# Attention, mixer and MLP on one core: where the output projection is staged, and how many attention outputs are buffered

## The chip, the cores and the metric

One core of a Trainium2 chip runs the whole program in one launch. The metric is the device time of an execution in microseconds (us); the kernel before has a median of 846.66 us over six runs (845.64 to 852.13).

## What is computed

The input x has 2048 rows of 576 numbers. After a layer norm, two branches are computed, and the output is x plus their product:

```python
xn = _layernorm(x, axis=-1)
s = _A_ref(xn, A_k_cache, A_v_cache, A_wq, A_wo)                # attention
g = _silu(_B_ref(xn, B_w1, B_w2, B_w3, B_w4))                   # mixer and MLP
return x + s * g
```

Branch A: queries `xn @ wq` for 32 heads of width 128; two query heads share one of 16 K and V heads; only the last 512 cached positions are used; softmax; the heads' outputs, side by side, times `wo` (4096 x 576). Branch B: a second layer norm, `gelu(... @ w1)`, four column groups of it shifted by 1 or 2 rows up or down, `@ w2`, plus its input (this is x1); then layer norm, `gelu(... @ w3)` to 4608 columns, `@ w4`, plus x1.

## The kernel before, in words

The rows are worked on in NB = 4 blocks of QB = 512 (TB = 4 tiles of 128 rows). Stage A (lines 216 to 697) does attention, the output projection and the mixer for all blocks; stage B (lines 700 to 991) does the MLP and the final product, with s, g and x1 passed through DRAM.

**The head loop.** Stage A is one loop over u = 0 ... 127 (line 679), u = 32 * block + head; "head u" below is a turn of it. The order on SP, POOL and TensorE is the order of the program (`manual_schedule`, line 662); VectorE and ScalarE are ordered by the framework's priorities, where `high_priority` (lines 391, 423, 501 and others) lets work in front. One turn runs:

- `stage_s(u, 0..3)` (line 398): four score products `sc` and on ScalarE four exponentials into `pT`;
- `stage_q(u + 1)` (line 382): the next head's query, five products `psq`, and its copy to qT, by VectorE in block 0 and by ScalarE in the others;
- `stage_v(u - 1)` (line 410), in two halves: 16 products `po` of 129 columns (the last is the row sum) into one of two PSUM buffers; VectorE takes the reciprocal (L424) and writes the scaled result into `o` (L425), a tile of `o_pool`, which has 4 buffers;
- `stage_t(u - 1)` (line 430): a DMA transpose on SP's queue, `oT<-o` (L433). `oT_pool` has 36 tiles. When it has landed, the `o` buffer is free.

**Filler.** Two tables put other work in: `fill` (`at`, `later`) for what is not TensorE's and `pe_fill` (`pe`) for TensorE's, which is cut into thirds behind the turn's later score products. Lines 615 to 659 are a timetable by head:

- the output projection of block b - 1 (`wo_atoms`, line 438), five groups at heads base + 1 to base + 5 of block b: four of 32 products `pswo`, each followed by a ScalarE copy (L454), and one of 128 narrow products `pswr` for the last 64 columns (copy L461), then the store of the tile `s_out` to s_dram (L462), on SP's queue, for the last block on ScalarE's. It reads the 32 oT of its block;
- the mixer's layer norm at base + 7 (`ln2_steps`), its transposes `xnnT<-xnn_b` (`tr2`, L357) on SP's queue at base + 10 to 13, its first product `b1` (`ph`, L492) from base + 15 or 17 on, which needs all four;
- `b2_shift` and `b2` (L543), which write x1 into a tile of `x1_pool` (2 buffers) that is stored to x1_dram (L570);
- the next block's x loads, layer norm (`ln1_steps`) and transposes `xT_b<-xn_b` (`tr1`, L357). For block 1 the layer norm starts at head 20 and the transposes stand at heads 23 to 26;
- loads on POOL's queue, some gated (`late`, line 303) by a small POOL copy that waits for a given head's first exponential: `load_wo(i)` for head 4 + 3i, and `load_wq`, `load_v`, `load_k`, which wait for their buffer.

`x1_pool` is used in turn for four K loads (`load_k`, block 0), for x1 of each block (line 535), and for x1 read back (`load_x1`). `hb_pool` (2 buffers) holds the mixer's gelu output `hb` of each block. `so_pool` has one buffer, for `s_out`.

Of the kernel before, what the change touches and what calls it, by code (L numbers as in the profile page):

```python
# [8 lines left out]
P = 128  # L9
# [3 lines left out]
BF16 = mybir.dt.bfloat16  # L13
# [18 lines left out]
def kernel(  # L32
# [18 lines left out]
    _, S, D = A_x.shape  # L51
# [10 lines left out]
    QB = 512  # L62
    NB = S // QB
    TB = QB // P
# [11 lines left out]
    PAD = 2  # L76
# [19 lines left out]
    def rows(ap, t0, n):  # L96
        return ap[t0 * P:(t0 + n) * P, :].rearrange("(tt p) d -> p tt d", p=P)
# [98 lines left out]
    x1_pool = ctx.enter_context(tc.tile_pool(name="x1_pool", bufs=2))  # L196
# [19 lines left out]
    with ExitStack() as actx:  # L216
        def pool(name, bufs, space=None):
            kw = {} if space is None else {"space": space}
            return actx.enter_context(tc.tile_pool(name=name, bufs=bufs, **kw))
# [14 lines left out]
        xraw = pool("xraw", 4)  # L234
        qT_pool = pool("qT_pool", 3)
        pT_pool = pool("pT_pool", 10)
        o_pool = pool("o_pool", 4)
        hb_pool = pool("hb_pool", 2)
        hs_pool = pool("hs_pool", 1)
        g1_pool = pool("g1_pool", 1)  # L240
        so_pool = pool("so_pool", 1)
        oT_pool = pool("oT_pool", 36)
        wo_sb = pool("a_wo", 1).tile([P, Hq, D], BF16, name="wo_sb")

# [8 lines left out]
        def load_x(b, eng):  # L253
            x_t[b] = []
            for tt in range(TB):
                xt = xraw.tile([P, D], BF16, name="xt")
                t = b * TB + tt
                eng.dma_start(out=xt[:], in_=x2[t * P:(t + 1) * P, :])
                x_t[b].append(xt)
# [43 lines left out]
        def late(ap, fn):  # L303
            g = nc.gpsimd.tensor_copy(out=gate[:, :], in_=ap)
            with tc.issue_after(g.ins):
                fn()
# [49 lines left out]
        def transpose_tile(dstT, src, tt):  # L356
            nc.sync.dma_start(out=dstT[:, :, tt * P:(tt + 1) * P], in_=src[:, tt, :], transpose=True)  # L357
# [14 lines left out]
        def tr1(b, tt):  # L372
            transpose_tile(xT_b[b % 2], xn_t[b], tt)
# [62 lines left out]
        so_t = {}  # L436

        def wo_atoms(qb):
            psp, tag = (ps_pq, "pq") if qb == NB - 1 else (ps_wo, "wo")
            groups = []  # L440
            st = {}

            def mm(ps, h, tt, lo, hi):
                nc.tensor.matmul(ps, lhsT=oT_t[qb * Hq + h][:, tt, :], rhs=wo_sb[:, h, lo:hi], start=(h == 0),  # L444
                                 stop=(h == Hq - 1))

            def main(tt, h):
                if tt == 0 and h == 0:
                    so_t[qb] = so_pool.tile([P, TB, D], BF16, name="s_out")
                if h == 0:  # L450
                    st["ps"] = psp.tile([P, M0], FP32, name="pswo", tag=tag)
                mm(st["ps"][:, :], h, tt, 0, M0)
                if h == Hq - 1:
                    nc.scalar.activation(out=so_t[qb][:, tt, 0:M0], in_=st["ps"][:, :], func=ACT.Copy, scale=0.5)  # L454

            def rem(tt, h):
                if tt == 0 and h == 0:
                    st["pr"] = psp.tile([P, TB, R0], FP32, name="pswr", tag=tag)
                mm(st["pr"][:, tt, :], h, tt, M0, D)
                if tt == TB - 1 and h == Hq - 1:  # L460
                    nc.scalar.activation(out=so_t[qb][:, :, M0:D], in_=st["pr"][:, :, :], func=ACT.Copy, scale=0.5)  # L461
                    (nc.scalar if qb == NB - 1 else nc.sync).dma_start(out=rows(s_dram, qb * TB, TB),  # L462
                                                                       in_=so_t.pop(qb)[:])

            for tt in range(TB):
                groups.append([lambda tt=tt, h=h: main(tt, h) for h in range(Hq)])
            groups.append([lambda tt=tt, h=h: rem(tt, h) for tt in range(TB) for h in range(Hq)])
            return groups

# [3 lines left out]
        def ln2_steps(b):  # L473
            return layernorm_steps(small, [xnn_b[:, tt, 0:D] for tt in range(TB)],
                                   [xn_t[b][:, tt, 0:D] for tt in range(TB)])

        def tr2(b, tt):
            transpose_tile(xnnT, xnn_b, tt)

        def b1(b, c):  # L480
            st = {}

            def mm(kc):
                if kc == 0:
                    if c == 0:
                        hb_t[b] = hb_pool.tile([P, 5, QB + 2 * PAD], BF16, name="hb")
                        if b == 0:
                            nc.vector.memset(hb_t[b][:, :, 0:PAD], 0.0)
                        if b == NB - 1:
                            nc.vector.memset(hb_t[b][:, :, PAD + QB:], 0.0)  # L490
                    st["ph"] = ps_pq.tile([P, QB], FP32, name="ph", tag="pq")
                nc.tensor.matmul(st["ph"][:, :], rhs=xnnT[:, kc, :],  # L492
                                 lhsT=w1r_sb[:, kc, :] if c == 4 else w1_sb[:, kc, c * c4:c * c4 + P],
                                 start=(kc == 0), stop=(kc == NDC - 1))
                if kc == NDC - 1:
                    gelu1(b, c, st["ph"])

            return [lambda kc=kc: mm(kc) for kc in range(NDC)]
# [25 lines left out]
        def b2_shift(b):  # L524
            with tc.high_priority(offset=HP):
                b2_shift_(b)
# [18 lines left out]
        def b2(b, tt):  # L545
            st = {}

            def mm(c):
                if c == 0:
                    st["ps"] = ps_wo.tile([P, M0], FP32, name="psx1", tag="wo")  # L550
                b2_mm(st["ps"][:, :], b, tt, c, 0, M0)
                if c == 4:
                    with tc.high_priority(offset=HP):
                        nc.vector.tensor_tensor(out=x1o_t[b][:, tt, 0:M0], in0=st["ps"][:, :],
                                                in1=xn_t[b][:, tt, 0:M0], op=ALU.add)

            return [lambda c=c: mm(c) for c in range(5)]
# [38 lines left out]
        def at(u, fn):  # L596
            fill.setdefault(u, []).append(fn)

        def pe(u, atoms):
            pe_fill.setdefault(u, []).extend(atoms)  # L600
# [5 lines left out]
        def later(u, make, per):  # L606
            cell = []
            for i in range(2 * TB + 1):
                def step(i=i):
                    if not cell:  # L610
                        cell.append(make())
                    cell[0][i]()
                at(u + i // per, step)

        for b in range(NB):
            base = b * Hq
            if b > 0:
                for i, group in enumerate(wo_atoms(b - 1)):
                    pe(base + 1 + i, group)
            later(base + 7, lambda b=b: ln2_steps(b), 3)  # L620
            for tt in range(TB):
                at(base + 10 + tt, lambda b=b, tt=tt: tr2(b, tt))
            for c in range(5):
                pe(base + (15 if 0 < b < NB - 1 else 17) + c, b1(b, c))
            for bb in ([b - 1] if b > 0 else []) + ([b] if b == NB - 1 else []):
                o2 = base + (28 if bb == b else 23 if b == NB - 1 else 21)
                at(o2 - 1, lambda bb=bb: b2_shift(bb))
                for tt in range(TB):
                    pe(o2 + tt, b2(bb, tt))
                pe(o2 + 3, b2_rem(bb))  # L630
            if b + 1 < NB:
                at(base + (8 if b == 0 else 4), lambda b=b: late(pT_t[b * Hq + (8 if b == 0 else 4)][0][0:1, 0:1],
                                                                 lambda: load_x(b + 1, nc.gpsimd)))
                u1 = base + (24 if b else 20)
                later(u1, lambda b=b: ln1_steps(b + 1), 3)
                for tt in range(TB):
                    at(u1 + (3 + tt // 2 if b else 3 + tt), lambda b=b, tt=tt: tr1(b + 1, tt))
        for i, group in enumerate(wo_atoms(NB - 1)):
            pe(U + 1 + i, group)
        at(2, lambda: late(pT_t[2][0][0:1, 0:1], load_w1))  # L640
# [59 lines left out]
    with ExitStack() as bctx:  # L700
# [181 lines left out]
        with tc.manual_schedule(engines={PE, DVE, ACTE}):  # L882
# [7 lines left out]
            for d in range(0, ND, 2):  # L890
                b = d // NP
# [4 lines left out]
                if end:  # L896
                    assert not work
                    bs = bs_pool.tile([P, TB, D], FP32, name="bs")
                    x1 = x1_t[b]
# [48 lines left out]
            b = NB - 1  # L948
# [34 lines left out]
            tt = TB - 1  # L983
# [11 lines left out]
    with tc.If(flag > 0):  # L995
        with ExitStack() as gctx:
# [19 lines left out]
            with tc.For_i(0, NT, 1) as t:  # L1016
# [10 lines left out]
                for h in range(Hq):  # L1027
                    g = h // REP
                    if h % REP == 0:
                        k_nat = work.tile([P, KCH, Dh], BF16, name="r_k")  # L1030
                        nc.sync.dma_start(out=k_nat[:],
                                          in_=A_k_cache[0, g, K0:, :].rearrange("(kc p) d -> p kc d", p=P))
                        v_g = work.tile([P, KCH, Dh], BF16, name="r_v")
                        nc.sync.dma_start(out=v_g[:],
                                          in_=A_v_cache[0, g, K0:, :].rearrange("(kc p) d -> p kc d", p=P))
# [16 lines left out]
                    p = work.tile([P, W], BF16, name="r_p")  # L1052
# [63 lines left out]
```

## Time and profile before

| what | us |
|---|---|
| median of the six runs | 846.66 |
| the six runs | 845.66, 845.64, 847.04, 850.60, 852.13, 846.27 |
| the profiled execution | 858.82 |
| its span, first to last instruction | 857.0 |
| TensorE busy in it | 829.6 |
| ScalarE, VectorE, POOL busy | 461.0, 426.1, 76.7 |

The profiled execution is longer than all six runs shown; times below that come from it are its own. Its mean granted TensorE clock is 0.992.

How such a page is read: a group's line gives source line, engine, operation, output<-input by the program's names, shapes and count, then busy time and mean ns of one, then the idle time of the engine just before these instructions and what ended most of it. "SPq" is a DMA issue on SyncE's queue. A line of waits gives who waited for whom, then total us, times and the longest. A line of the timeline gives the start, the length, the engine and the operation, merged where equal ones follow each other; in brackets stands the idle time before it and what ended it. "DMA to landing" is the time from a transfer's issue to its arrival.

In the stretch of stage A over blocks 1 to 3 (180 to 566 us) TensorE's waits for other engines and DMAs add up to 1 us, and in stage B, from 566 us to the last products, to 0.2 us. Of the transposes `oT<-o` the median lands 3.0 us after its issue, the longest 17.4; of `xnnT<-xnn_b` 5.4 and 19.6.

### The profile page before, as it was taken

The page shows a single profiled execution, that of the slowest core. Times are in us where ns is not written, and L with a number is a line of the kernel's source. Part 1 is how long each engine was busy: PE and PEld are TensorE (multiplying, and loading weights), DVE is VectorE, ACT ScalarE, POOL GpSimd, SP SyncE. Part 2 cuts the span into 40 slices and gives each one's busy share as a digit, 9 for nine tenths or more (in the row PEclk, how much of TensorE's full clock was granted, in tenths as well). Part 3 has the DMA queues.
Part 4 walks back from the last instruction along what each step waited for, and adds up shares of the span by engine and source line. Part 5 has one row for each costly group of instructions (what it writes and reads, how often), then busy time and mean ns, then how long its engine had stood idle before and what let it go on. Part 6 is the DMA issues. An engine that isn't in the chain of part 4 may idle for free.

```text
span 857.0 us, 19361 instructions
## 1 busy us (share of the span) xinstructions
PE 829.6 (97%) x7896; PEld 487.1 (57%) x7980; DVE 426.1 (50%) x1351; ACT 461.0 (54%) x825; POOL 76.7 (9%) x134
## 2 busy tenths in 40 slices
PE   8978989999999999999999999999999999999996
PEld 6645655566565566565466556455555555555554
DVE  5755961156772145873126686025236636655333
ACT  5754774378885368877359876023333424334610
POOL 3431210310101101010001000000000000000000
PEclk9998999999999999999999999999999999999999
DMA  7997582245355137245128424995001321230101
GB/s 179 220 191 128 148 160 58 71 102 116 93 112 92 47 87 130 66 121 96 41 60 138 99 66 98 255 329 144 2 2 43 53 77 43 39 92 15 44 15 45
DMA packets 139983, 83.94 MB, mean 98 GB/s; under 512 B 106944, under 2 KB 133248, under 8 KB 139888
## 3 DMA queue, kind: packets, MB, share of 16 engines
q1 hardware_dynamic: 130048, 53.01, 30.8%
q0 software_dynamic: 8448, 28.15, 12.3%
q10 hardware_dynamic: 1392, 1.48, 0.5%
q8 instruction: 64, 1.05, 0.5%
q14 instruction: 31, 0.25, 0.1%
HBM read 49.17 MB, written 9.44 MB: 68 GB/s over the span
## 4 chain that ended last, share of the span: by engine, by line


## 5 line engine op out<-in xcount | busy, mean ns | idle before, releaser
L405 ACT ACTIVATE pT<-sc 128x512 bf16<-128x512 f32 x512 | 290.4, 596 | 115.6 <-PE sc L403 100.3
L403 PE MATMUL sc<-qT,kT 128*128 128x512 bf16 x493 | 176.3, 381 | 1.3 <-DVE qT L393 0.6
L420 PEld LDWEIGHTS <-pT 128*128 128x128 bf16 x2048 | 140.8, 98 | 62.7 <-DVE o L425 12.4
L420 PE MATMUL po<-v_sb,pT 128*128 128x129 bf16 x2048 | 163.2, 222 | 12.4 <-DVE o L425 10.9
L388 PE MATMUL psq<-xT_b,wq_b 128*128 128x512 bf16 x603 | 152.0, 379 | 2.8 <-DMA xT_b<-xn_b 0.7
L424 DVE RECIPROCAL ri_b<-po 128x2 f32<-128x2 f32 x256 | 42.9, 168 | 190.4 <-PE po L420 186.5
L769 PE MATMUL ph<-xT_b,w_s 64*128 64x512 bf16 x976 | 127.1, 376 | 0.0
L806 PE MATMUL pm<-w_s,h 64*128 64x512 bf16 x864 | 122.3, 377 | 0.0
L425 DVE TENSOR_TENSOR o<-po,ri_b 128x256 bf16<-128x256 f32 x256 | 107.7, 421 | 24.1 <-DMA oT<-o 17.7
L444 PE MATMUL pswo<-wo_sb,oT 128*128 128x512 bf16 x497 | 114.2, 379 | 0.8
L787 ACT ACTIVATE h<-ph 128x512 bf16<-128x512 f32 x67 | 39.4, 597 | 130.5 <-PE ph L769 130.5
L388 PEld LDWEIGHTS <-wq_b 128*128 128x128 bf16 x640 | 62.5, 98 | 75.3 <-issue 3.5
L806 PEld LDWEIGHTS <-h 64*128 64x128 bf16 x1728 | 70.8, 94 | 55.6 <-issue 0.4
L444 PEld LDWEIGHTS <-oT 128*128 128x128 bf16 x1024 | 64.9, 98 | 55.2
L806 PE MATMUL pr<-w_s,h 64*128 64x64 bf16 x864 | 90.2, 189 | 0.2 <-ACT h L787 0.2
L769 PEld LDWEIGHTS <-w_s 64*128 64x128 bf16 x1152 | 57.2, 94 | 48.2 <-issue 0.2
L395 ACT ACTIVATE qT<-psq 128x512 bf16<-128x512 f32 x96 | 57.4, 598 | 28.4 <-PE psq L388 27.0
L785 DVE COPY hx<-ph 128x512 f32<-128x512 f32 x55 | 38.0, 691 | 69.3 <-PE ph L769 69.3
L403 PEld LDWEIGHTS <-kT 128*128 128x128 bf16 x512 | 47.7, 98 | 28.4 <-DVE qT L393 1.2
L265 POOL DMA_DIRECT2D wq_b<-in_A_wq_dram x30 | 23.4, 778 | 315.4 <-PE psq L388 296.1
L787 ACT ACTIVATE h<-hx 128x512 bf16<-128x512 f32 x55 | 34.6, 630 | 7.9 <-DVE hx L785 6.0
L759 DVE TENSOR_SCALAR fence<-ph,ph 1x1 f32<-1x1 f32 x61 | 12.8, 209 | 51.2 <-PE ph L769 50.6
(122 smaller groups left out, 643.0 us busy)
## 6 DMA issues: line engine op xcount, KB each, us to landing
wq_b<-in_A_wq_dram POOLq DMA_DIRECT2D x30, 512.0 KB, 5.4
w_s<-in_B_w_dram SPq DMA_DIRECT2D x9, 576.0 KB, 6.9
wo_sb<-in_A_wo_dram POOLq DMA_DIRECT2D x8, 576.0 KB, 5.2
w_s<-in_B_w_dram SPq DMA_DIRECT2D x9, 512.0 KB, 7.8
x_dram<-x SPq DMA_DIRECT2D x4, 576.0 KB, 3.5
x<-x_dram SPq DMA_DIRECT2D x4, 576.0 KB, 5.3
s_b<-s_dram SPq DMA_DIRECT2D x4, 576.0 KB, 5.3
x_b<-in_A_x_dram SPq DMA_DIRECT2D x4, 576.0 KB, 5.6
```

The costliest lines, as they stand in the source:

```text
L388: nc.tensor.matmul(psq[:, :], lhsT=w[:, kc, hh * Dh:(hh + 1) * Dh], rhs=xT_b[qb % 2][:, kc, :], start=(kc == 0), stop=(kc == NDC - 1))
L395: nc.scalar.activation(out=qT[:, :], in_=psq[:, :], func=ACT.Copy)
L403: nc.tensor.matmul(sc[:, :], lhsT=kT[:, g, kc * P:(kc + 1) * P], rhs=qT_t[u][:, :], start=True, stop=True)
L405: nc.scalar.activation(out=pT[:, :], in_=sc[:, :], func=ACT.Exp, scale=SCALE)
L420: nc.tensor.matmul(po[:, j, :], lhsT=pTs[kc][:, tt * P:(tt + 1) * P], rhs=v_sb[:, g, kc, 0:Dh + 1], start=(kc == 0), stop=(kc == KCH - 1))
L424: nc.vector.reciprocal(out=ri, in_=po[:, :, Dh])
L425: nc.vector.tensor_tensor(out=o[:, t0:t0 + 2, :], in0=po[:, :, 0:Dh], in1=ri.unsqueeze(2).to_broadcast([P, 2, Dh]), op=ALU.mult)
L444: nc.tensor.matmul(ps, lhsT=oT_t[qb * Hq + h][:, tt, :], rhs=wo_sb[:, h, lo:hi], start=(h == 0), stop=(h == Hq - 1))
L769: nc.tensor.matmul(ps[i][:, :], lhsT=lhsT, rhs=xT[half, kc, :], start=first, stop=last, skip_group_check=True)
L785: nc.vector.tensor_copy(out=src[:, :], in_=ps[i][:, :])
L787: nc.scalar.activation(out=h3[:, :], in_=src[:, :], func=ACT.Gelu_apprx_tanh)
L806: nc.tensor.matmul(out, lhsT=h3_t[b, fc][half, tt * P:(tt + 1) * P], rhs=w4_s[fc // WS][half, fc % WS, lo:hi], start=key not in started, s ...
```

## The change

- `o_pool` has eight buffers instead of four.
- `so_pool` is gone. The projection of blocks 0 to 2 is staged in a tile of `x1_pool`, that of block 3 in a tile of `hb_pool`, seen as 4 x 576. Copies and stores stay as they are.
- Block 0's projection stands at heads 34 to 38 instead of 33 to 37.
- Block 1's first layer norm starts at head 19 instead of 20, and its transposes stand at heads 24 to 27 instead of 23 to 26.

```diff
-        o_pool = pool("o_pool", 4)
+        o_pool = pool("o_pool", 8)
         hb_pool = pool("hb_pool", 2)
         hs_pool = pool("hs_pool", 1)
         g1_pool = pool("g1_pool", 1)
-        so_pool = pool("so_pool", 1)
...
             def main(tt, h):
                 if tt == 0 and h == 0:
-                    so_t[qb] = so_pool.tile([P, TB, D], BF16, name="s_out")
+                    if qb == NB - 1:
+                        so = hb_pool.tile([P, 5, QB + 2 * PAD], BF16, name="hb")[:].rearrange("p a b -> p (a b)")
+                        so_t[qb] = so[:, 0:TB * D].rearrange("p (t d) -> p t d", t=TB)
+                    else:
+                        so_t[qb] = x1_pool.tile([P, TB, D], BF16, name="x1")
...
                     (nc.scalar if qb == NB - 1 else nc.sync).dma_start(out=rows(s_dram, qb * TB, TB),
-                                                                       in_=so_t.pop(qb)[:])
+                                                                       in_=so_t.pop(qb)[:, :, :])
...
             if b > 0:
                 for i, group in enumerate(wo_atoms(b - 1)):
-                    pe(base + 1 + i, group)
+                    pe(base + (2 if b == 1 else 1) + i, group)
...
-                u1 = base + (24 if b else 20)
+                u1 = base + (24 if b else 19)
                 later(u1, lambda b=b: ln1_steps(b + 1), 3)
                 for tt in range(TB):
-                    at(u1 + (3 + tt // 2 if b else 3 + tt), lambda b=b, tt=tt: tr1(b + 1, tt))
+                    at(u1 + (3 + tt // 2 if b else 5 + tt), lambda b=b, tt=tt: tr1(b + 1, tt))
```

## The prediction

> **What bounds the kernel now.** I read the page first, for shares. VectorE's product `o` (L425) is one of the few operations there whose idle time ends with a DMA.
>
> ```profile
> PE 829.6 (97%) x7896; PEld 487.1 (57%) x7980; DVE 426.1 (50%) x1351; ACT 461.0 (54%) x825; POOL 76.7 (9%) x134
> L425 DVE TENSOR_TENSOR o<-po,ri_b 128x256 bf16<-128x256 f32 x256 | 107.7, 421 | 24.1 <-DMA oT<-o 17.7
> ```
>
> TensorE is busy for 97% of the span, so only a hole in TensorE can be won. TensorE's waits come next (total, times, longest):
>
> ```profile
> PE po L420 <- DVE o L425: 10.9, 3, 5.9
> ```
>
> Every other wait of TensorE is 1.6 us or less. So three waits of the attention's second product, for `o`, which waited for a transpose to leave its buffer, are all that this change can touch. Cut into time, they are at 58, 69 and 115 us. The windows (length, busy us by engine with instructions, granted clock, DMA share, GB/s):
>
> ```profile
> 58.30:64.30 6.00, 0.15 (x1) 0.00 (x0) 0.47 (x2) 0.60 (x1) 0.00 (x0) 0.74 1.00 126
> 64.30:69.30 5.00, 4.99 (x29) 3.13 (x29) 1.22 (x4) 1.79 (x3) 0.30 (x2) 0.63 1.14 129
> 115.00:117.50 2.50, 0.06 (x1) 0.00 (x0) 0.42 (x2) 0.60 (x1) 0.00 (x0) 1.00 0.66 126
> ```
>
> Then TensorE's timeline over the first two holes, and the SP queue's over the same stretch, in which oT and xnnT transposes alternate:
>
> ```profile
> 58.08 0.38 PE L403 MATMUL sc<-qT,kT 128*128 128x512 bf16 x1
> 64.31 1.05 PE L420 MATMUL po<-v_sb,pT 128*128 128x129 bf16 x8 [5.86 <-DVE o L425]
> ...
> 71.91 1.05 PE L420 MATMUL po<-v_sb,pT 128*128 128x129 bf16 x8 [2.57 <-DVE o L425]
> ...
> 76.64 0.81 PE L492 MATMUL ph<-xnnT,w_sb 128*128 128x512 bf16 x3
> ```
>
> ```profile
> 48.22 2.65 SPq L433 DMA_TRANSPOSE oT<-o  x1
> 50.96 2.92 SPq L357 DMA_TRANSPOSE xnnT<-xnn_b  x1
> 53.97 3.41 SPq L433 DMA_TRANSPOSE oT<-o  x1
> 57.43 4.91 SPq L357 DMA_TRANSPOSE xnnT<-xnn_b  x1
> 62.43 3.43 SPq L433 DMA_TRANSPOSE oT<-o  x1
> 65.92 4.86 SPq L357 DMA_TRANSPOSE xnnT<-xnn_b  x1
> 70.87 17.81 SPq L433 DMA_TRANSPOSE oT<-o  x7
> ```
>
> The rows follow each other without a gap: SP waits for no producer here, it is held by the DMA engines. The median transpose issue takes 1.19 us; here it takes 2.7 to 4.9. The oT of 48.22 (head 9) lands 15.5 us later, at 63.7, when `o` of head 13, which has its buffer, goes on. The xnnT of 65.92, the last quarter that the mixer's first product (L492) needs, lands 9.6 us later, at 75.5. L492 starts at 76.64, only 1.1 us after that. This last fact decides most of what follows.
>
> **What the holes cost.** Undisturbed, TensorE would go on at 58.30, take 3.10 us for a head with K transposes (52.31 to 55.41), 2.88 for one without (55.41 to 58.29), and reach L492 0.47 later, at 64.75. It got there at 76.64: 11.9 us lost, 8.6 of it waiting, the rest mostly reduced clock. The third hole (115.06 to 117.56) costs 2.5. Together 14.4 us. The profiled execution took 858.82 (span 857.0 and 1.8 around it), so without holes it would take 844.4. The median of the six runs shown is 846.66, the lowest 845.64: if the rest is the same, they hold only about 2.2 and 1.2 us of holes, and the two longest (850.60, 852.13) 6.2 and 7.7. So the profile shows a bad case, and the gain has to be taken against 2.2, not against 14.4.
>
> **The change part by part.**
>
> Eight `o` buffers. Head u's `o` now waits for the transpose of head u-8 instead of u-4. At the first hole that is head 5, landed long before; at the third it is head 18 instead of 22, which sat behind an xT_b transpose for which SP had waited until 110.42 (VectorE's apply). All three waits at L425 go: up to 14.4 us in this execution, about 2.2 in a median one. What is late next: L492, for xnnT. Its transposes stand in the same order on SP in both kernels, and no buffer makes them land sooner. With the profile's DMA load TensorE comes to L492 at 64.75 and waits 10.75 us there.
>
> How early the DMA load allows L492: between oT of head 9 and the last xnnT SP issues five more transposes, and TensorE needs 64.75 - 57.8 = 6.95 us between their uses, 1.4 us per issue. At the undisturbed 1.19 to 1.27 us the xnnT is not late; at the profile's 3 to 5 it is 4.75 us later than the oT was.
>
> Two rules of the Trainium skill speak against the change. "DMA: Bandwidth & Descriptors", section "Issuing engines are not separate DMA queues": transfers of SP and GpSimd run on the same 16 engines and interleave. POOL's load gate of head 16, at 68.69 here, opens some 7 us sooner when TensorE isn't held; its 832 KB (one wo, two v) then fall ahead of the last xnnT. Were the queues apart, this would cost nothing; by the rule it delays xnnT by 832 KB at 286 GB/s (the window from 71.9) to 126 GB/s (58.3 to 64.3): 2.9 to 6.6 us. I count it only where the DMAs are as full as here. "TensorE: Matmul & The Clock Gate", section "What's actually happening": an idle window of about 3.4 us halves the clock until about as much work has been done. The rows agree in kind (0.63 behind 6.0 us idle, 1.00 beside 2.5). By the rule a restart costs 1.7 us; by the row 1.9 (5.03 us for the head of 3.10). One long wait at L492 pays it once; I take 1.9.
>
> Staging in x1 and hb. The same 16 copies of 597 ns and 4 of 384 ns on ScalarE and the same four stores of 576 KB remain: nothing by themselves. The waits move: block 0's copy waits for K loads and transposes 15 heads old; each later x1 tile takes the buffer of a tile stored at least 10 heads before (a store lands in 3.4 to 8.1 us, a head takes 2.9); the last block's copy in hb waits for block 2's shift, done before. Following each wait of the built program to its partner, none but `o`'s own has a partner less than ten heads old that it had not before, apart from an h3 tile of the MLP's sixth pair that waits for the last store: it lands at about 575, and the pair (3.9 us each from 566.4) comes at about 586. Taken at 0; if that cover were gone it would cost at most the 8.1 us of the store. The w loads of stage B stand in the same order with the same partners.
>
> Block 0's wo a head later. TensorE does the same 256 matmuls in another place. Heads 32 and 33 are then both without filler, in which ScalarE (4 x 596 + 598 = 2.98 us) is a little slower than TensorE (2.88): 0.1 us. Against that, oT of head 31 (issued at 131.2, landed at 133.7) gets one more head. On SP, oT of head 36 now waits for the remainder group one head later (its buffer is head 0's), just ahead of the s_dram store, which before held SP for 10.2 us at the same place; what queues behind (oT 37 to 40) then needs its `o` buffer only eight heads on. Sum between -0.2 and +0.3; I take 0.
>
> LN of block 1 a head sooner, its transposes a head later. VectorE's order shows the four applies still behind head 25, half a head nearer together; SP's row order has oT of head 22 ahead of them. The last xT_b was issued at 118.70 and landed 2.6 later, 121.3; TensorE wanted it at 125.01, and will want it at 122.5. It holds with 1.2 us to spare; 0 to 1.5 us if DMA is fuller. Taken at 0.
>
> Sum for the median execution: 846.66 - 2.2, and about 0.5 of L492 left: **844.9**. Its own range is 843.2 (if the third hole's 2.5 us sits in every run and the hole-free time is lower than the profile's) to 846.2.
>
> **The rivals.** *The wait moves to L492 whole.* For it: the 1.1 us between the last xnnT's landing and L492. Against: the third hole isn't of this kind, and most runs hold far less than the profile. Then 846.7, no change. The change then does what it says and the time doesn't follow. *Slower.* The earlier gate of head 16 fills the DMAs ahead of the last xnnT, and TensorE waits cold at L492. Price with the profile's load: 10.75 + (2.9 to 6.6) + 1.9 - 14.4 = 1.2 to 4.9 us lost. It decides the median only if the earlier loads bring the median run to where the two long ones are: 850.6 to 852.1 and a little, say 853. *Faster by more.* Below 842.4 some 2 us of other idle time would have to go; TensorE's matmuls run at clock 1.00 everywhere else, so only the start could give it: 842.
>
> **How the numbers follow.** Forecast 0.52, wait moved whole 0.28, slower 0.15, faster by more 0.05. 0.5% is 4.2 us, about what a measurement of this kernel can tell from no change: 842.4 to 850.9. The first two lie within: 0.80. The range leaves out the last two (0.20 together) and ends at the shorter of the two long runs: 843.0 to 850.6.
>
> **What would show it.** Right: no wait of L425 for oT and none of L420 for L425; TensorE through 58 to 64 without a hole; whatever wait is left ends at L492, by xnnT. Third step right: no hole at 115, and none at L388 for xT_b. Wrong: a wait for an x1 or hb buffer on ScalarE, a wait at L444 for oT near head 34, an idle TensorE in the MLP stage; or a time under 842, by which the hole-free time worked out here would be too high.

## The result and the profile after

| | median | executions | lowest to highest | 847 us or less |
|---|---|---|---|---|
| kernel before, beside it | 848.31 | 74 | 845.12 to 862.95 | 16 |
| kernel after | 843.69 | 37 | 842.94 to 858.84 | 32 |

The ratio is 0.9944 [0.9931, 0.9957]: 0.56% less time (0.43 to 0.69%), small but clear of no change. The profiled execution took 845.06 (span 843.3, clock 0.998). Medians, counts and extremes here and below are over all executions, while ratios leave out the slowest ones (over 1.5% above the fastest of their kernel). The kernel before has medians of 848.3 to 851.5 in the four sets of its runs, so each kernel's ratio is to the runs of before made beside it.

The page's line of busy times and VectorE's product `o`, now L424:

```profile
PE 827.0 (98%) x7896; PEld 486.3 (58%) x7980; DVE 427.7 (51%) x1351; ACT 460.8 (55%) x825; POOL 76.7 (9%) x134
L424 DVE TENSOR_TENSOR o<-po,ri_b 128x256 bf16<-128x256 f32 x256 | 107.9, 421 | 6.5 <-DVE ri_b L423 0.3
```

The work is the same; the 24.1 us of idle time before `o`, 17.7 of it ended by a transpose, have become 6.5, none of it ended by one. TensorE's waits, the longest first (total, times, longest):

```profile
PE warm L672 <- POOL ident masks.py:199: 1.6, 1, 1.6
PE ps_k L291 <- DMA x<-in_A_k_cache_dram: 0.8, 1, 0.8
PE sc L402 <- DVE qT L392: 0.6, 1, 0.6
```

No wait for `o` is left. The same three windows as before, by the clock of this execution:

```profile
58.30:64.30 6.00, 5.95 (x55) 3.86 (x55) 4.10 (x12) 4.58 (x9) 1.82 (x4) 1.00 1.29 196
64.30:69.30 5.00, 5.00 (x40) 2.88 (x38) 3.31 (x10) 3.03 (x6) 0.62 (x1) 1.00 1.14 275
115.00:117.50 2.50, 2.50 (x25) 1.66 (x24) 1.33 (x6) 2.28 (x6) 0.00 (x0) 1.00 0.51 100
```

TensorE is busy through all three at clock 1.00. The DMA share is as high as before, but the engines move 196 and 275 GB/s where they moved 126 and 129. The SP queue shows the other half:

```profile
51.65 1.53 SPq L432 DMA_TRANSPOSE oT<-o  x1
53.24 1.28 SPq L356 DMA_TRANSPOSE xnnT<-xnn_b  x1
54.60 1.51 SPq L432 DMA_TRANSPOSE oT<-o  x1
56.17 1.43 SPq L356 DMA_TRANSPOSE xnnT<-xnn_b  x1
57.69 11.43 SPq L432 DMA_TRANSPOSE oT<-o  x5
```

An issue takes 1.3 to 1.5 us here and took 2.7 to 4.9 in the execution profiled before. So two things differ between the two profiles: the change, and how slow the transposes happened to be. The last xnnT lands 9.0 us after 56.17, at 65.2, and its reader stands next in TensorE's timeline:

```profile
65.74 0.81 PE L495 MATMUL ph<-xnnT,w_sb 128*128 128x512 bf16 x3
```

Some 0.6 us lie between them. Stage B's first product starts at 552.3 instead of 566.4. From there to the last start of the MLP's first product it takes 247.7 us against 247.4: the whole difference of the two profiles, 13.8 us, lies in stage A. But the medians differ by 4.6 only, so a comparison of the two profiles alone would overstate the change three times.

The lowest executions, 845.12 and 842.94, differ by 2.2 us. That is the size of the third hole, near head 26, as other profiles of the timetable of before show it below (1.9 to 2.3).

### The profile page after: what moved, and what is told of

It reads as the page before. It is cut to its first block, busy times and chain, and to the rows that moved or that the text cites. A ratio compares the mean times of both kernels' runs of the same rounds, so it can differ in the third digit from the quotient of the medians.

```text
span 843.3 us, 19365 instructions
## 1 busy us (share of the span) xinstructions
PE 827.0 (98%) x7896; PEld 486.3 (58%) x7980; DVE 427.7 (51%) x1351; ACT 460.8 (55%) x825; POOL 76.7 (9%) x134
## 4 chain that ended last, share of the span: by engine, by line
## 5 line engine op out<-in xcount | busy, mean ns | idle before, releaser
L419 PE MATMUL po<-v_sb,pT 128*128 128x129 bf16 x2048 | 161.4, 220 | 1.3 <-ACT pT L404 0.3
L772 PE MATMUL ph<-xT_b,w_s 64*128 64x512 bf16 x976 | 127.1, 376 | 0.2 <-DVE hx L788 0.2
L424 DVE TENSOR_TENSOR o<-po,ri_b 128x256 bf16<-128x256 f32 x256 | 107.9, 421 | 6.5 <-DVE ri_b L423 0.3
L772 PEld LDWEIGHTS <-w_s 64*128 64x128 bf16 x1152 | 57.1, 94 | 48.7 <-issue 0.5
```

Of the source, the lines that this page charges most:

```text
L419: nc.tensor.matmul(po[:, j, :], lhsT=pTs[kc][:, tt * P:(tt + 1) * P], rhs=v_sb[:, g, kc, 0:Dh + 1], start=(kc == 0), stop=(kc == KCH - 1))
L424: nc.vector.tensor_tensor(out=o[:, t0:t0 + 2, :], in0=po[:, :, 0:Dh], in1=ri.unsqueeze(2).to_broadcast([P, 2, Dh]), op=ALU.mult)
L772: nc.tensor.matmul(ps[i][:, :], lhsT=lhsT, rhs=xT[half, kc, :], start=first, stop=last, skip_group_check=True)
```

## The experiments

The theory: TensorE idles at two places. Near head 14 (the first two holes of the prediction) the cause is slow transposes beside the weight loads; near head 26 (its third hole) it is the order of SP's queue. Buffers cure both, and the staging only makes room. The rivals: the timetable does it; the staging costs something; the wait goes on to the mixer's first product.

The order of the queue, in the profile before: SP waits 9.8 us for VectorE, until block 1's normalized rows are there for the first xT_b transpose, and oT of head 22 stands behind it. The view names `o`, VectorE's operation that came last; in the run with the projection's move alone, below, the first of the layer norm's applies ends at 98.78 and SP issues the transpose at 98.81.

```profile
SPq L357 <- DVE o L425: 9.8, 1, 9.8
```

```profile
110.42 1.20 SPq L357 DMA_TRANSPOSE xT_b<-xn_b  x1
111.67 1.29 SPq L433 DMA_TRANSPOSE oT<-o  x1
```

### Eight buffers and staging, the timetable of before

```diff
-                    pe(base + (2 if b == 1 else 1) + i, group)
+                    pe(base + 1 + i, group)
-                u1 = base + (24 if b else 19)
+                u1 = base + (24 if b else 20)
-                    at(u1 + (3 + tt // 2 if b else 5 + tt), lambda b=b, tt=tt: tr1(b + 1, tt))
+                    at(u1 + (3 + tt // 2 if b else 3 + tt), lambda b=b, tt=tt: tr1(b + 1, tt))
```

> The changed kernel with the timetable of before (block 0's projection at heads 33 to 37, block 1's layer norm at head 20, its transposes at 23 to 26): eight o buffers and the new staging alone. Theory (the whole gain is the wait of L424's product for the transpose that leaves its buffer): 843.7 us, ratio to before 0.994, no wait of po for o in the profile, no hole at head 26 either. Rival (the timetable is half of it or more): 846 us or above, with a hole near head 26 or a wait of the projection for oT near head 33.

Measured: 843.67 (842.86 to 850.15, 9 executions), ratio 0.9938 [0.9901, 0.9976]; no wait for `o`, as expected. The buffers, with the staging that makes room for them, give all that the change gives. Three of the nine took 847.4 to 850.2; they weren't profiled.

### Staging alone: four buffers, the timetable of before

```diff
-        o_pool = pool("o_pool", 8)
+        o_pool = pool("o_pool", 4)
```

(and the timetable as above)

> Staging in x1 and hb alone: four o buffers and the timetable of before. Theory: nothing, 848 us, ratio 1.000 within 0.002; waits of po for o as before, two near head 14 and one near head 26. Rival (staging costs or gains by itself, by a wait of ScalarE for a buffer or by other addresses): off by 0.3% or more.

Measured: 857.93 (853.94 to 871.23, 13), ratio 1.0085 [1.0054, 1.0116]. No effect was expected; it is slower, by a wait that neither kernel has. TensorE's waits:

```profile
PE ph L772 <- ACT h L790: 6.8, 1, 6.8
PE po L419 <- DVE o L424: 2.3, 1, 2.3
```

The second is the hole near head 26. The first stands at the start of the MLP. ScalarE's timeline there:

```profile
554.64 0.38 ACT L464 ACTIVATE hb<-pswr 128x256 bf16<-128x256 f32 x1 [3.14 <-PE pswr L443]
555.06 0.46 ACTq L465 DMA_DIRECT2D s_dram<-hb  x1
563.73 1.28 ACT L790 ACT_TABLE_LOAD   x1 [8.70 <-DMA w_s<-in_B_w_dram]
565.02 0.60 ACT L790 ACTIVATE h<-ph 128x512 bf16<-128x512 f32 x1
```

The bracket names a weight load, but ScalarE goes on at 563.73, and the store `s_dram<-hb` of 555.06 lands 8.7 us after its issue, at 563.8. By the built program's addresses, which no trace shows, the MLP's first h3 tile (the gelu's output) lies where this `hb` tile lay, so writing it waits for the store to have read it. With `o_pool` at four, stage B's tiles lie elsewhere than in the kernel after.

### Staging alone, with 4 KB per partition of unused space behind `o_pool`

```diff
+        pool("pad", 1).tile([P, 4 * TB * Dh], BF16, name="pad")
```

> Staging alone once more (four o buffers, timetable of before), with an unused tile of 4 KB per partition behind the o buffers, so that all later tiles lie where they lie in the changed kernel. Staging alone was slower, by a wait of 6.8 us at the start of the MLP stage: its first h3 tile lies on the block 3 staging, and waits for the store. Theory (addresses, not staging): that wait is gone and the time is that of before, ratio 0.998 to 1.002. Rival (storing from hb is itself slower): ratio 1.006 or more.

Measured: 849.56 (844.68 to 861.05, 22), ratio 0.9984 [0.9955, 1.0013]. The wait at L772 is gone, though every store, copy and weight load is as in the run before it; so it was where the tiles lie. That the h3 tile is the one concerned rests on the built program. What is left, `po` for `o`, is that of the kernel before:

```profile
PE po L420 <- DVE o L425: 2.6, 2, 2.2
```

Staging in x1 and hb has no cost that can be told from these runs, as long as the space falls as it does with eight buffers.

### The timetable alone, twice

Kernel before, with block 0's projection a head later and block 1's layer norm as after; four buffers, `so_pool`.

> The timetable moves alone, on the kernel before: four o buffers, s_out in its own tile. Theory: the transpose of head 22 now stands ahead of block 1's first xT_b transpose on SP, so that the hole near head 26 goes or is under 0.5 us; the two near head 14 stay. Gain 0.5 to 2.5 us, ratio 0.997 to 0.9995. Rival (the timetable carries the gain): ratio 0.994 to 0.995.

Measured: 844.3 (843.35 to 862.76, 9, eight of them at most 846.44), ratio 0.992 [0.989, 0.9951]; of the waits for `o` 0.8 us remained, near head 26 (106.6 us), and none near head 14. A smaller gain was expected (at most 0.997); this was as good as the whole change, the rival's forecast and more. So it was run again later, beside other runs of before:

> The kernel before with the whole timetable of after (block 1's normalization at head 19, block 0's output projection a head later) and four buffers, once more. Theory (four buffers leave the wait near head 14 open, the timetable only cures the one near head 26): executions fall into two groups, 843 to 845.5 and 848 to 852, as with the normalization's move alone, median 844 to 849. Rival (the timetable cures both): at least eight of nine under 846.5 as in the first look, median 844.3.

Measured: 846.58 (843.91 to 863.86, 22), ratio 0.9971 [0.9945, 0.9996]. Twelve of 22 were at most 847, the others 849.2 to 863.9, so the executions do fall into groups; 843 to 845.5 was too narrow for the lower one. Its profile (845.17) has no wait for `o` either, with four buffers, and 0.9 us at L492 for xnnT. The two intervals meet only between 0.9945 and 0.9951, and nine executions are few. So the rival that the timetable alone does as much as the buffers isn't excluded: it all but removes the hole near head 26, and what it does near head 14 isn't settled.

### The layer norm's move alone

```diff
-                u1 = base + (24 if b else 20)
+                u1 = base + (24 if b else 19)
-                    at(u1 + (3 + tt // 2 if b else 3 + tt), lambda b=b, tt=tt: tr1(b + 1, tt))
+                    at(u1 + (3 + tt // 2 if b else 5 + tt), lambda b=b, tt=tt: tr1(b + 1, tt))
```

> On the kernel before, only block 1's layer norm a head sooner and its transposes a head later; the projection stays. Theory, after the timetable alone was as fast as the whole change: what an ordinary execution of before loses is the hole near head 26, where the transpose of head 22 stands behind block 1's first xT_b transpose, and this move is what cures it: ratio 0.992 to 0.995. Rival (the projection's move does it, by more time for oT of head 31): ratio 0.999 to 1.001.

Measured: 849.02 (843.21 to 859.3, 14), ratio 0.996 [0.9929, 0.999]. The two holes in TensorE's timeline:

```profile
68.34 0.64 PE L420 MATMUL po<-v_sb,pT 128*128 128x129 bf16 x8 [4.10 <-DVE o L425]
68.82 1.12 PE L492 MATMUL ph<-xnnT,w_sb 128*128 128x512 bf16 x3
...
112.10 0.64 PE L420 MATMUL po<-v_sb,pT 128*128 128x129 bf16 x8 [0.46 <-DVE o L425]
```

The hole near head 26 has shrunk to 0.46: on SP, 23 oT now stand ahead of the first xT_b, 22 before. The one near head 14 is still there, and the ratio is above the forecast 0.992 to 0.995, though its interval reaches into it. Five of the 14 executions lie at 843.2 to 845.6, the others at 848.9 and above. In this one the last xnnT, issued at 55.89, landed 12.3 us later, at 68.2, only 0.6 us before L492 started.

### Block 0's projection a head later, alone

```diff
-                    pe(base + 1 + i, group)
+                    pe(base + (2 if b == 1 else 1) + i, group)
```

> On the kernel before, only block 0's projection a head later. Theory: nothing, ratio 0.999 to 1.001. Rival (the projection's move carries the gain): ratio 0.992 to 0.995.

Measured: 847.67 (845.61 to 863.73, 22), ratio 0.9979 [0.9955, 1.0002]; its profile holds the wait near head 26 alone, 1.9 us. No gain that can be told from none. The lowest of 22 is 845.6, which fits the hole near head 26 being in all of them; only one was profiled.

### The kernel before once more

> The kernel before, unchanged, for another look at where an execution of it idles. Theory: a hole near head 26 of 2 to 6 us in this one too; holes near head 14 only if the execution is one of the long ones (over 852 us). Rival (the holes near head 14 are the ordinary loss): holes there, and little near 26.

Measured: 850.05 (846.03 to 857.55, 10), ratio 0.9995; profiled at 853.61. Both holes again:

```profile
69.04 0.69 PE L420 MATMUL po<-v_sb,pT 128*128 128x129 bf16 x8 [4.70 <-DVE o L425]
69.53 1.48 PE L492 MATMUL ph<-xnnT,w_sb 128*128 128x512 bf16 x3
...
112.01 0.64 PE L420 MATMUL po<-v_sb,pT 128*128 128x129 bf16 x8 [2.30 <-DVE o L425]
```

And SP's queue ahead of the first:

```profile
53.48 3.12 SPq L433 DMA_TRANSPOSE oT<-o  x1
56.66 1.28 SPq L357 DMA_TRANSPOSE xnnT<-xnn_b  x1
```

L492 follows the first hole at once. In this execution the last xnnT was issued at 56.66 and landed 12.3 us later, at 69.0: if it lands no sooner with more buffers, TensorE would come to L492 4.7 us sooner and wait there for some 4.1 of them. In such an execution the wait would nearly all move, and the same holds for the one of the layer norm's move alone (3.5 of 4.1).

### Five buffers

```diff
-        o_pool = pool("o_pool", 8)
+        o_pool = pool("o_pool", 5)
```

> The changed kernel with five o buffers instead of eight. Theory: one buffer more than before is one head (2.9 us) more patience. The hole near head 26 (2.5 us in the profile of before) goes; of the one near head 14 (6.0 us there) 2.9 us go. 844.5 us, ratio 0.995 to 0.997, in a profile with slow transposes a wait of po for o of up to 3 us is left. Rival (it is not the buffer's age but the placement): as before, or as with eight.

Measured: 847.15 (843.02 to 860.62, 22), ratio 0.9945 [0.9924, 0.9967]. Ten lie at 843.0 to 846.0, ten at 847.0 to 849.6, two at 860: one more buffer reaches the lowest times, but not as often as eight in the runs of the kernel after (32 of 37 at most 847). The median is above the forecast 844.5, the ratio just below its range; beside the same runs of before, 0.9945 can't be told from the 0.9938 of eight buffers. Its profile (844.45) has no wait for `o` and 0.3 us at L495 for xnnT.

### The weight loads pulled together, eight buffers

```diff
-            at(4 + 3 * i, lambda i=i: late(pT_t[4 + 3 * i][0][0:1, 0:1], lambda: load_wo(i)))
+            at((4, 7, 10, 11, 12, 13, 14, 15)[i], lambda i=i: late(pT_t[(4, 7, 10, 11, 12, 13, 14, 15)[i]][0][0:1, 0:1], lambda: load_wo(i)))
```

> The kernel after, with the loads of block 0's projection weights pulled together: gates at heads 4, 7, 10, 11, 12, 13, 14 and 15 in place of every third head, so that about 1.7 MB more falls into the heads in which the normalized input of the first mixer is transposed. Nothing else is changed. Theory (the DMA queues are the cause of the late transposes, and with eight buffers the wait of the attention product turns into a wait of the first mixer product): no wait of po for o; the last xnnT lands some 6 us later (1.7 MB at about 286 GB/s), and L495 waits 3 to 6 us for it; 846 to 851 us. Rival (the transposes are late for a reason that has nothing to do with loads): no wait at L495 over 1 us, 843 to 844.5 us.

Measured: 858.73 (854.92 to 859.72, 8), ratio 1.0101 [1.0066, 1.0136]. TensorE's waits:

```profile
PE ph L495 <- DMA xnnT<-xnn_b: 9.8, 1, 9.8
PE warm L672 <- POOL ident masks.py:199: 1.6, 1, 1.6
```

And SP's queue:

```profile
52.73 2.33 SPq L356 DMA_TRANSPOSE xnnT<-xnn_b  x1
55.15 10.60 SPq L432 DMA_TRANSPOSE oT<-o  x1
65.80 3.30 SPq L356 DMA_TRANSPOSE xnnT<-xnn_b  x1
```

One oT holds the queue for 10.6 us, and the last xnnT is issued at 65.80 instead of 56.17. The place and the kind are as expected, the size is larger (3 to 6 us and 846 to 851 were forecast). Of the loads pulled forward, two had been issued when this oT was, a third 0.3 us later and a fourth before the last xnnT. Counted as three, 1.77 MB cost 9.6 us, 184 GB/s and not 286. There is no wait for `o` even here, so this is the prediction's rival in full: the wait is at the mixer.

### The weight loads moved out of the way, four buffers

```diff
-            at(4 + 3 * i, lambda i=i: late(pT_t[4 + 3 * i][0][0:1, 0:1], lambda: load_wo(i)))
+            at((4, 7, 18, 20, 22, 24, 26, 28)[i], lambda i=i: late(pT_t[(4, 7, 18, 20, 22, 24, 26, 28)[i]][0][0:1, 0:1], lambda: load_wo(i)))
```

> The kernel before with its four buffers and its timetable, only the weight loads' gates moved out of the heads around the mixer's transposes: heads 4, 7, 18, 20, 22, 24, 26 and 28. Theory (transposes are slowed by loads beside them): the wait of the attention product for o near head 14 goes, also in the worse executions, and the one near head 26 stays at about 2 us or grows, since loads now lie there; 846 to 848 us, and next to no execution above 851. Rival (the transposes are late without the loads): as the kernel before, 846 to 855 with a median near 850.

Measured: 850.37 (849.17 to 855.14, 22), ratio 0.9998 [0.9976, 1.0019]. TensorE's longest wait:

```profile
PE po L420 <- DVE o L425: 4.5, 1, 4.5
```

It is the one near head 26, at 103.2 to 107.7, where the loads now lie. The one near head 14 is gone, the xnnT issues take 1.2 to 1.4 us, and 21 of 22 executions lie within 849.2 to 852.5, the narrowest spread of all. So in this kernel the loads beside the transposes make the hole near head 14 and most of the scatter. The expected level was missed by 2.4 us: the other hole doubled, and the clock behind it cost 2.2 us more.

### The same late loads, eight buffers

> The kernel after with the same late gates (4, 7, 18, 20, 22, 24, 26, 28). If loads beside the transposes make the tail of executions above 847 us, this one has none: 843.0 to 843.8 us with all executions under 846, and the last xnnT lands some us before L495 asks for it. Rival: as the kernel after, 843.7 with one execution in seven above 847.

Measured: 852.6 (843.51 to 857.53, 22), ratio 1.0013 [0.9986, 1.0041]. No execution above 846 was expected. This was meant as a better version, and it takes all of the gain away. Its profile is one of the shorter executions (848.89); in TensorE's timeline:

```profile
113.43 2.29 PE L387 MATMUL psq<-xT_b,wq_b 128*128 128x512 bf16 x5 [2.86 <-DMA xT_b<-xn_b]
```

Eight buffers cover `o`, but no buffer covers xT_b: block 1's first query waits for its own input, whose transposes now go beside the loads. In this kernel they also stand a head later than in the run before it, and what each of the two does wasn't separated. The last was issued at 108.21 and landed 5.2 us later; in the kernel after it was issued at 107.78 and landed 2.6 later, at 110.4. Only three of the 22 were at most 847. What the longer ones (849 to 858) wait for wasn't profiled. The narrow spread of the run before it doesn't come back. Gates that avoid both heads 10 to 16 and 22 to 28 weren't tried.

## Why the prediction was right, and where its sizes were off

**What the range shows.** 843.0 to 850.6 would have held an unchanged median, 848.31, as well, so that 843.69 lies in it says little of the mechanism. The waits say more.

**The bound and the waits that can go: right.** TensorE's busy time hardly moved (829.6 to 827.0), the three waits at L420 are gone, and nothing of stage B changed.

**What the holes cost: right for the profile, too small for the median.** The working gave 14.4 us for the profiled execution; the two profiles differ by 13.8, and where L492 was to be reached without a hole, 64.75, it was reached at 65.74 and, in the run with packed loads, would have been at 74.50 - 9.81 = 64.69. The hole-free time came out as 844.4; the lowest executions of four kernels lie at 842.9 to 843.2 and the median after at 843.69. The term that failed is "about 2.2" us of holes in a median execution. It was 846.66, a median of six, less 844.4. Over 74 executions the median before is 848.31, so it holds 848.3 - 843.7 = 4.6 us that the change takes away. The six (1.7 us too low) and the hole-free time (0.7 too high) both make the term too small. The six drop out of 844.9 itself, which is the hole-free 844.4 and the 0.5 for L492: these two make it 1.2 too high. But they spoil the gain: 1.8 us was forecast and 4.6 came.

**The third hole.** The range's lower end allowed for "the third hole's 2.5 us sits in every run". It does in every profile with four buffers and that part of the timetable as before: 2.5 in the profile of before and 2.3, 2.3, 2.2, 1.9 and, with late loads, 4.5 us in five others. The times agree. With this hole no execution of any kernel lies below 844.68; without it, packed loads aside, the lowest are 842.9 to 843.9. I should have seen it: that hole has a cause in the program (SP waits for VectorE's apply with oT of head 22 behind it), while the first two have one in the DMA load. A hole made by order was in every profile; one made by load was in some.

**The buffers: right in what goes, but only half of the gain is traced.** With them alone, all of the gain. What is late next is L492 (now L495), as said: with 0.6 us to spare in the profile after, 0.9 us late in the second run of the timetable, 9.8 with packed loads. The third hole accounts for some 2.2 us of the 4.6. The rest should be the holes near head 14. But in the three profiled executions that have one above half a microsecond, the last xnnT landed 0.5 to 1.1 us before L492 started (75.5, 69.0 and 68.2 against 76.64, 69.53 and 68.82), so by these traces buffers could win no more than that there. What is on record is that long executions became rarer: 26 of the 74 before lie above 849.5 (847 and the third hole's 2.5), 5 of the 37 after above 847. No profile shows how.

**How early the DMA load allows L492: wrong in its measure.** The working took the issue time for the cause, and at 1.2 to 1.3 us per issue the xnnT was not to be late. In two executions with a hole near head 14, six of the seven issues took 1.2 to 1.7 us and one 2.6 or 3.1; what was long was the landing, 12.3 us for the last xnnT against 9.0 in the profile after. (Its 4.75 us should be 4.85: 10.75 less 63.7 - 57.8.)

**The staging: taken at 0, and 0 within 0.9955 to 1.0013.** The cover named for it (the tile that waits for the last store comes only in the sixth pair) is what the price depends on. With four buffers the tile falls into the first pair, the cover is gone, and 6.8 us of waiting follow; "at most the 8.1 us of the store" was a fair bound: the store took 8.7 us here, TensorE saw 6.8 of it, and the two staging profiles, 853.94 and 846.75, differ by 7.2.

**Block 0's projection: 0, and nothing that can be told from it.** Ratio 0.9979 [0.9955, 1.0002] alone.

**The layer norm's move: taken at 0, wrong by itself.** I saw in SP's row order that oT of head 22 now stands ahead of xT_b and looked only at the price, the margin of xT_b. Alone it takes the third hole down from 2.3 to 0.46 us and the ratio to 0.996. In the sum it made no difference, because the eight buffers cure the same hole: 0.9938 with the buffers alone, 0.9944 with both. The margin was judged well: "1.2 us to spare", and 0.8 in the profile after (landed at 110.4, wanted at 111.20). "If DMA is fuller" became the run with late loads, at 2.9 us.

**The rule on queues.** The Trainium skill, "DMA: Bandwidth & Descriptors", section "Issuing engines are not separate DMA queues", says that transfers of different engines share the same 16 DMA engines and interleave. At the rates of the profile before, the estimate was that 832 KB on POOL's queue delay SP's transposes by 2.9 to 6.6 us. In the profile after, the load behind head 16's gate was issued at 62.66, when the last xnnT had been issued 6.5 us before; it landed at 65.2, and what that load did to it can't be read off. Where loads do come ahead, the rule holds and the price is of that size: 9.6 us for 1.77 MB is 4.6 for 832 KB, an estimate (6.9 or 3.5 if two or four loads count). By separate queues it would have been nothing.

**The rule on the clock.** "TensorE: Matmul & The Clock Gate", section "What's actually happening", gave an estimate of 1.7 us for a restart (half of 3.4), the row 1.9. The clock behind the wait of 9.8 us (windows of 2 us: busy times of the engines, then granted clock, DMA share, GB/s):

```profile
74.50:76.50 2.00, 2.00 (x8) 0.90 (x9) 0.00 (x0) 0.04 (x1) 0.00 (x0) 0.50 0.55 99
76.50:78.50 2.00, 2.00 (x12) 1.18 (x11) 0.97 (x3) 0.56 (x1) 0.00 (x0) 0.50 0.24 46
78.50:80.50 2.00, 2.00 (x11) 0.98 (x10) 1.36 (x4) 1.19 (x2) 0.00 (x0) 0.73 0.34 66
80.50:82.50 2.00, 2.00 (x23) 1.41 (x22) 1.65 (x5) 1.38 (x3) 1.80 (x3) 1.00 0.22 47
```

2 x (0.50 + 0.50 + 0.27) = 2.5 us lost. Reckoned in the same way it was 2.2 behind the 4.5 us of the late loads with four buffers, 1.7 behind the 4.7 of the kernel before once more, 1.4 behind the 6.8 of the staging alone and 1.6 behind the 2.9 of the late loads with eight buffers. Row and rule were near; the loss doesn't grow with the wait in these five.

**The rivals.** The wait that moves to L492 whole isn't what the median execution does. That it is what the longer ones do (three of nine with buffers alone, the ten of 22 with five buffers at 847.0 to 849.6) is argued from where xnnT landed in executions with four buffers; none of these was itself profiled. The slower case needs about 10 us of lateness, as the packed loads show. Faster by more did not come: 843.69 is above its 842.4. The gain of 0.56% is still past half a per cent, not by that rival's mechanism: no other idle time went, the median execution before was only longer than the six told.

**What stays open:** what makes up the 2.4 us of the median's gain beyond the third hole's 2.2, since no execution of the kernel before near its median was profiled; why the transposes are slow in one execution and not in the next with the same program, and so how often the hole near head 14 falls out with four buffers (one of nine above 847 in one run of the timetable, ten of 22 in the other).

## What to carry to other kernels

Sort the holes of a profile by cause before pricing them: here the one made by the order of a queue was in every profile, the one made by the load in some, and a single profile, or six executions, shows the second kind too large or too small. When a wait for a buffer goes, ask which reader stands next in that queue and how much margin it has (here 0.6 us for the mixer's and 0.8 for the next block's transposes), since loads moved into those margins cost all of the gain. Sharing a buffer across stages cost nothing that could be measured, but what a later stage waits for depended on where its tiles lie, and that moved with the size of one pool.

## What the runs showed that was not expected

- The DMA engines are as full in a bad stretch as in a good one (shares 1.00 and 1.14 against 1.29 and 1.14) but move about half as much, 126 and 129 against 196 and 275 GB/s. The share doesn't tell one from the other. The issue times on SP do between these two (2.7 to 4.9 against 1.3 to 1.5 us), but not in general: two executions with a hole near head 14 had issues of 1.2 to 1.7 us but for one. There the time to landing does, 12.3 us for the last xnnT against 9.0.
- A wait of 2.5 us for the attention's second product left the clock at 1.00; one of 2.86 us, with late loads, brought it to 0.50 for about 3 us.
- The store `s_dram<-hb` took 8.7 us to land amid 335 GB/s of weight loads, the three earlier stores of the same size 3.5 to 5.
